# The norm of the next token group on VectorE: made a group early, in the order of the program

## Chip, cores, metric

One core of a Trainium2 chip. The metric is the device time of one execution in microseconds (us), median over runs. A profile gives a span, which is about 1.9 us shorter than the time of the same run. Line numbers such as L190 are lines of the kernel that a trace belongs to, so the same line of code has another number in each kernel.

## The reference

The output is `x + A(norm(x)) + B(norm(x))` for 2048 tokens of width 512. A is linear attention with 32 heads of width 16, B an MLP of width 1792 with the activation mish.

```
xn  = (x - mean) / sqrt(var + 1e-5)
q, k, v = split(xn @ wqkv);  pq, pk = per head q @ w_phi, k @ w_phi
phi = concat(softmax(p), softmax(-p))            # for q and k
kv  = sum over tokens of phi_k^T v;  z = sum over tokens of phi_k
A   = (phi_q @ kv / (phi_q @ z + 1e-6)) @ wo
B   = mish(xn @ w1 + b1) @ w2
```

kv and z need all tokens before any output exists. So the kernel has a first phase over 4 groups of 512 tokens (4 tiles of 128 each) and then a second phase that makes the outputs.

## The kernel before

A group of the first phase makes, on TensorE, `pk` (keys folded with w_phi), `pv` (values), `pq`, seven pairs of `ph` (the MLP) and `pkv` (the sum over tokens). ScalarE does the exponentials `ek` and `eqT` and mish. VectorE makes, for each tile, the sums `ss`, the reciprocals `rk` and the products `v12`, which `pkv` reads; it also does the norm: statistics `st`, their aggregates `mv`, the reciprocal root `rstd` (on GpSimd for groups 1 to 3), the scaled tile `xn` and its transpose `xnT` (made by a DMA for groups 1 to 3). To fold is to multiply w_phi into the weights once, at the start (`pf`); `pnd` and `po` are matmuls of the second phase. A scheduler orders the instructions of each engine, unless `follow` chains them:

```python
def follow(key, ins):            # orders ins behind the last instruction with the same key
    ...tc.add_manual_dep(ins.ins, prev.ins.name, <order only, no wait>)...

def stage_ln(g):
    ...
    for t in range(TPG):
        st = spool.tile(...)
        follow("dve", nc.vector.bn_stats(st[:], xg[:, t, :]))
        nc.vector.bn_aggr(mv[:, t, :], st[:])
    ...                          # g > 0: 1/sqrt(var + eps) of all four tiles on GpSimd
    for t in range(TPG):
        xn = xnpool.tile([P, D], BF16, name="xn")            # pool of 4
        nc.vector.tensor_scalar(out=xn[:], in0=xg[:, t, :], ...subtract mean, times rstd...)
        if g > 0:
            nc.sync.dma_start_transpose(out=xnT[:, t], in_=xn[:])

def finish(ek):                  # returned by v_pair; pvs are two PSUM banks of a pool of 2
    for tt in range(2):
        nc.vector.reduce_sum(ss[:], ek[:, :, tt, :]...)
        nc.vector.reciprocal(rk[:], ss[:])
        nc.vector.tensor_tensor(out=v12[...], in0=pvs[tt]..., in1=rk..., op=ALU.mult)

for g in range(NG):
    # [cut] g = 0: v_pair, fold of wq, two k_pair
    ek0 = k_pair(xnT, 0); ek1 = k_pair(xnT, 1)
    v0, vfin = v_pair(xnT, 0);  vfin(ek0)
    q_pair(g, xnT, 0); q_pair(g, xnT, 1)
    h_pair(xnT, acts[g], 0)
    v1, vfin = v_pair(xnT, 1);  vfin(ek1)
    if g + 1 < NG:
        xnTs[g + 1], _ = stage_ln(g + 1)                     # written here, placed by the scheduler
    for fp in range(1, 4): h_pair(xnT, acts[g], fp)
    stage_kvacc(g, parts)                                    # pkv, then kvacc on VectorE
    for fp in range(4, 7 or 6): h_pair(xnT, acts[g], fp)
```

The softmax here doesn't subtract the row's maximum and nothing guards it: scores larger than these inputs give would overflow.

Of the kernel before, what the change touches and what calls it, by code (L numbers as in the profile page):

```python
# [17 lines left out]
def kernel(  # L18
# [12 lines left out]
    nc = tc.nc  # L31
# [38 lines left out]
    nc.scalar.dma_start(wk_raw[:], wqkv_v[:, :, D : 2 * D])  # L70
    wv = wts.tile([P, KT, D], BF16, name="wv")
    nc.sync.dma_start(wv[:], wqkv_v[:, :, 2 * D : 3 * D])
    Wsrc = prep_w.tile([P, 4, DH], BF16, name="Wsrc")
    with nc.allow_non_contiguous_dma(reason="tiny w_phi load"):
        nc.scalar.dma_start(Wsrc[:], wphi_v)
# [48 lines left out]
    wqp = wts.tile([P, KT, D], BF16, name="wqp")  # L124
    wkp = wts.tile([P, KT, D], BF16, name="wkp")
# [38 lines left out]
    def rstd_of(g, rstd, mv):  # L164
        if g == 0:
            follow("act", nc.scalar.activation(rstd, mv, ACT.Sqrt, bias=eps_t[:]))
            nc.vector.reciprocal(rstd, rstd)
        else:
            nc.gpsimd.tensor_scalar(
                out=rstd, in0=mv, scalar1=1e-5, scalar2=None, op0=ALU.add  # L170
            )
            nc.gpsimd.tensor_tensor(out=rstd, in0=rstd, in1=mhalf[:], op=ALU.pow)

    def stage_ln(g):
        xg = xgs[g]
        mv = spool.tile([P, TPG, nc.vector.BN_AGGR_DIM], FP32, name="mv")
        rstd = spool.tile([P, TPG], FP32, name="rstd")
        xnT = xnTpool.tile([P, TPG, KT, P], BF16, name="xnT")
        xns = []
        for t in range(TPG):  # L180
            st = spool.tile([P, nc.vector.BN_STATS_DIM], FP32, name="st")
            follow("dve", nc.vector.bn_stats(st[:], xg[:, t, :]))  # L182
            nc.vector.bn_aggr(mv[:, t, :], st[:])
            if g == 0:
                rstd_of(g, rstd[:, t : t + 1], mv[:, t : t + 1, 1])
        if g > 0:
            rstd_of(g, rstd[:], mv[:, :, 1])
        for t in range(TPG):
            xn = xnpool.tile([P, D], BF16, name="xn")
            nc.vector.tensor_scalar(  # L190
                out=xn[:],
                in0=xg[:, t, :],
                scalar1=mv[:, t, 0:1],
                scalar2=rstd[:, t : t + 1],
                op0=ALU.subtract,
                op1=ALU.mult,
            )
            xns.append(xn)
            if g > 0:
                nc.sync.dma_start_transpose(out=xnT[:, t], in_=xn[:])  # L200
        return xnT, xns

    def ln_T(xnT, xns):
        if True:
            ptr = big("ptr", [P, TPG, KT, P], BF16)
            for t in range(TPG):
                for kt in range(KT):
                    pe(
                        nc.tensor.transpose(
                            ptr[:, t, kt, :], xns[t][:, kt * P : (kt + 1) * P], ident[:]  # L210
                        )
                    )
            nc.scalar.copy(xnT[:, 0:2], ptr[:, 0:2])
            nc.vector.tensor_copy(xnT[:, 2:4], ptr[:, 2:4])
# [11 lines left out]
    def fold_T(src, engines):  # L226
# [11 lines left out]
        for jh, copy in enumerate(engines):  # L238
            ins = copy(wT[:, 2 * jh : 2 * jh + 2, :], ptr[:, 2 * jh : 2 * jh + 2, :])
            if src is wq_raw and jh == 0:  # L240
                follow("act", ins)
        return wT

    def fold_mm(wT, dst):
        for kp in range(KT // 2):
            pf = big("pf")
            for kk in range(2):
                kt = 2 * kp + kk
                for j in range(4):
                    pe(nc.tensor.matmul(  # L250
                        pf[:, kk, j * P : (j + 1) * P],
                        lhsT=wT[:, j, kt * P : (kt + 1) * P],
                        rhs=Wbd[:, j, :],
                        start=True,
                        stop=True,
                    ))
            follow("dve", nc.vector.tensor_copy(dst[:, 2 * kp, :], pf[:, 0]))
            follow("act", nc.scalar.copy(dst[:, 2 * kp + 1, :], pf[:, 1]))


    def k_pair(xnT, pr):
        pk = big("pk")
        for tt in range(2):
            for kt in range(KT):
# [3 lines left out]
                    rhs=wkp[:, kt, :],  # L268
# [7 lines left out]

    def v_pair(xnT, pr):
        pvs = []
        for tt in range(2):
            pv = bank_v("pv")  # L280
            for kt in range(KT):
                pe(
                    nc.tensor.matmul(  # L283
                        pv[:],
                        lhsT=xnT[:, 2 * pr + tt, kt, :],
                        rhs=wv[:, kt, :],
                        start=(kt == 0),
                        stop=(kt == KT - 1),
                    )
                )  # L290
            pvs.append(pv)
        v12s = []

        def finish(ek):
            for tt in range(2):
                ss = spool.tile([P, 2, NH], FP32, name="ss")
                nc.vector.reduce_sum(  # L297
# [3 lines left out]
                )  # L301
                rk = spool.tile([P, 2, NH], FP32, name="rk")
                nc.vector.reciprocal(rk[:], ss[:])  # L303
                v12 = vpool.tile([P, 2, NH, VW], BF16, name="v12")
                nc.vector.tensor_tensor(  # L305
# [6 lines left out]
                )  # L312
# [275 lines left out]
```

## Time and profile before

| | before |
|---|---|
| time, 3 runs | 196.21 us median (195.61 to 197.53) |
| span of the profiled run, and its time | 195.2 us, 197.05 us |
| TensorE / VectorE / ScalarE busy | 181.2 / 119.0 / 107.9 us |
| mean granted TensorE clock | 0.983 |

The page's summary of the chain that ended last, by engine, reads:

```profile
PE 75%; ACT 7%; DVE 7%; DMA 5%; issue 2%; SPq 2%; POOL 1%; ACTq 0%; DVEq 0%; POOLq 0%
```

The chain is followed back from the last instruction; a share is time in which that engine (PE is TensorE, DVE is VectorE, ACT is ScalarE) held up the end. Three quarters are TensorE's own work. The prediction below shows where the rest lies. Its lines are read so: a line of the chain has start, length, engine, what; a line of the timeline adds shapes, the number of instructions, and in brackets how long the engine sat idle before and for whom; a line of the waits has the total, the number of waits and the longest. Some matmul records are missing from a trace, so a count such as x7 can stand for 8.

### The profile page before, as it was taken

To read this page: it belongs to the slowest core of one execution; us is meant where nothing else is said; L and a number is where in the kernel's file an instruction comes from. 1 tells how busy PE (TensorE), PEld (TensorE's weight loads), DVE (VectorE), ACT (ScalarE), POOL (GpSimd) and SP (SyncE) were. 2 spreads that over 40 slices of the span, in tenths; PEclk is the share of its full clock that TensorE was granted. 3 is DMA by queue.
4 is the path that set the end of the run, shared out by engine and by line. 5 is a ranking of instruction groups with operands and counts; after the bars stand their busy time and mean duration, and the time that the engine had idled before them with its cause. 6 is when DMAs were issued, how large, how long until landed. Compare 5 with 4: busy or idle time off the path is not lost.

```text
span 195.2 us, 2791 instructions
## 1 busy us (share of the span) xinstructions
PE 181.2 (93%) x1034; PEld 90.7 (46%) x1051; DVE 119.0 (61%) x233; ACT 107.9 (55%) x175; POOL 14.0 (7%) x35
## 2 busy tenths in 40 slices
PE   7779999999189999999999999999999999999992
PEld 2355446444034644446444464445555555555440
DVE  1948999364894203982039864897666677766600
ACT  3578976598704479974799855343322222333311
POOL 3200410202110000110001100000000000000000
PEclk9999999999958999999999999999999999999999
DMA  6999302619300013000000000138322632222220
GB/s 192 381 403 386 151 0 55 125 59 197 108 0 0 3 27 81 0 0 3 0 0 0 0 3 0 27 81 165 55 69 66 164 81 57 54 54 57 54 81 27
DMA packets 24233, 15.93 MB, mean 82 GB/s; under 512 B 16284, under 2 KB 23196, under 8 KB 24220
## 3 DMA queue, kind: packets, MB, share of 16 engines
q1 hardware_dynamic: 22636, 14.69, 27.4%
q10 hardware_dynamic: 1584, 1.07, 1.7%
q8 instruction: 8, 0.13, 0.3%
q14 instruction: 5, 0.04, 0.1%
HBM read 9.98 MB, written 2.10 MB: 62 GB/s over the span
## 4 chain that ended last, share of the span: by engine, by line
PE 75%; ACT 7%; DVE 7%; DMA 5%; issue 2%; SPq 2%; POOL 1%; ACTq 0%; DVEq 0%; POOLq 0%
PE ph L366 25%; PE po L453 22%; PE po L462 6%; PE pv L283 6%; PE pk L265 4%; PE pkv L326 4%; DMA Wsrc<-in_A_w_phi_dram 4%; PE pq L348 4%; PE pnd L390 4%; SPq L200 2%; ACT ek L274 1%; ACT ek L273 1%; ACT act L377 1%; DMA xnT<-xn 1%; DVE ss L297 1%
## 5 line engine op out<-in xcount | busy, mean ns | idle before, releaser
L366 PE MATMUL ph<-xnT,w_sb 128*128 128x512 bf16 x224 | 51.8, 386 | 0.4 <-ACT eqT L357 0.4
L453 PE MATMUL po<-w_sb,act 128*128 128x512 bf16 x216 | 51.2, 379 | 0.4
L377 ACT ACTIVATE act<-ph,b1f 128x512 bf16<-128x512 f32 x56 | 35.5, 684 | 27.4 <-PE ph L366 27.4
L366 PEld LDWEIGHTS <-w_sb 128*128 128x128 bf16 x224 | 22.2, 100 | 27.1 <-issue 2.9
L471 ACT CAST y<-po 128x512 bf16<-128x512 f32 x16 | 9.4, 586 | 44.4 <-PE po L462 44.4
L453 PEld LDWEIGHTS <-act 128*128 128x128 bf16 x224 | 21.3, 98 | 22.3
L297 DVE TENSOR_REDUCE ss<-ek 128x64 f32<-128x1024 bf16 x16 | 18.7, 1211 | 19.1 <-ACT ek L274 19.0
L422 DVE TENSOR_TENSOR on<-pnd,wd 128x512 f32<-128x512 f32 x32 | 20.6, 686 | 1.7
L283 PE MATMUL pv<-wv,xnT 128*128 128x512 bf16 x59 | 16.4, 408 | 5.0 <-DVE v L305 4.6
L305 DVE TENSOR_TENSOR v<-pv,rk 128x1024 bf16<-128x1024 f32 x16 | 18.3, 1188 | 0.0
L462 PE MATMUL po<-wo_sb,oT 128*128 128x512 bf16 x63 | 16.4, 379 | 0.1
L357 ACT ACTIVATE eqT<-pq 128x1024 bf16<-128x1024 f32 x16 | 15.1, 1040 | 0.7 <-PE pq L348 0.6
L182 DVE BATCH_NORM_STATS2 st<-xg 128x6 f32<-128x512 bf16 x16 | 10.4, 672 | 8.1 <-DMA xg<-in_A_x_dram 8.1
L348 PE MATMUL pq<-xnT,wqp 128*128 128x512 bf16 x64 | 14.5, 379 | 0.0
L265 PE MATMUL pk<-wkp,xnT 128*128 128x512 bf16 x61 | 14.3, 379 | 0.2
L407 DVE TENSOR_TENSOR td<-ds 128x64 f32<-128x64 f32 x16 | 3.6, 225 | 16.4 <-ACT ds L403 16.3
L283 PEld LDWEIGHTS <-xnT 128*128 128x128 bf16 x64 | 6.5, 103 | 13.0 <-issue 6.6
L390 PE MATMUL pnd<-kvm,eqT 128*128 128x144 bf16 x128 | 11.3, 226 | 0.5 <-DVE on L422 0.3
L390 PEld LDWEIGHTS <-eqT 128*128 128x128 bf16 x128 | 9.0, 98 | 5.9 <-DVE on L422 2.4
L313 POOL CAST v<-rk 128x64 bf16<-128x64 f32 x16 | 7.0, 458 | 64.5 <-DVE rk L303 64.5
L429 DVE TENSOR_TENSOR o_t<-on 128x512 bf16<-128x512 f32 x16 | 11.1, 692 | 0.5
L338 DVE TENSOR_TENSOR kvacc<-pkv,kvacc 128x544 f32<-128x544 f32 x6 | 4.3, 725 | 9.9 <-PE pkv L326 9.9
(63 smaller groups left out, 150.1 us busy)
## 6 DMA issues: line engine op xcount, KB each, us to landing
xg<-in_A_x_dram SPq DMA_DIRECT2D x8, 512.0 KB, 4.1
out_dram<-y SPq DMA_DIRECT2D x16, 128.0 KB, 2.1
w_sb<-in_B_w_dram SPq DMA_DIRECT2D x2, 896.0 KB, 9.9
w_sb<-in_B_w_dram SPq DMA_DIRECT2D x1, 1792.0 KB, 12.9
wk_raw<-in_A_wqkv_dram ACTq DMA_DIRECT2D x1, 512.0 KB, 5.1
wv<-in_A_wqkv_dram SPq DMA_DIRECT2D x1, 512.0 KB, 6.0
wq_raw<-in_A_wqkv_dram ACTq DMA_DIRECT2D x1, 512.0 KB, 10.1
wo_sb<-in_A_wo_dram SPq DMA_DIRECT2D x1, 512.0 KB, 13.5
```

The costliest lines, as they stand in the source:

```text
L265: pe(nc.tensor.matmul(pk[:, tt, :], lhsT=xnT[:, 2 * pr + tt, kt, :], rhs=wkp[:, kt, :], start=(kt == 0), stop=(kt == KT - 1),))
L283: nc.tensor.matmul(pv[:], lhsT=xnT[:, 2 * pr + tt, kt, :], rhs=wv[:, kt, :], start=(kt == 0), stop=(kt == KT - 1),)
L297: nc.vector.reduce_sum(ss[:], ek[:, :, tt, :].rearrange("p s (h e) -> p s h e", e=DH), axis=AX.X,)
L305: nc.vector.tensor_tensor(out=v12[:, :, :, 0:DH], in0=pvs[tt][:] .rearrange("p (o h e) -> p o h e", o=1, e=DH) .to_broadcast([P, 2, NH, DH ...
L348: pe(nc.tensor.matmul(pq[:, jj, :], lhsT=wqp[:, kt, j * P : (j + 1) * P], rhs=xnT[:, :, kt, :], start=(kt == 0), stop=(kt == KT - 1),))
L357: follow("act", nc.scalar.activation(eqT[:, sl, gs], pq[:], ACT.Exp, scale=sign))
L366: nc.tensor.matmul(ph[:, ff, :], lhsT=w1_sb[:, kt, f * P : (f + 1) * P], rhs=xnT[:, :, kt, :], start=(kt == 0), stop=(kt == KT - 1),)
L377: nc.scalar.activation(act[:, f, :], ph[:, ff, :], ACT.Mish, bias=b1f[:, f : f + 1])
L390: nc.tensor.matmul(pnd[:, j // 2, (j % 2) * 144 : (j % 2) * 144 + 144], lhsT=eqT[:, pl * 4 + j, tok0 : tok0 + P], rhs=kvm[:, pl * 4 + j], ...
L422: nc.vector.tensor_tensor(out=on[:, pl], in0=nds[pl][:, :, :, 0:DH], in1=wd[:, pl, :, :, None].to_broadcast([P, 2, 16, DH]), op=ALU.mult,)
L453: nc.tensor.matmul(po[:], lhsT=acts[g][:, f, t * P : (t + 1) * P], rhs=w2_sb[:, f, :], start=False, stop=False, skip_group_check=True,)
L462: nc.tensor.matmul(po[:], lhsT=oT[:, j, :], rhs=wo_sb[:, j, :], start=False, stop=(j == 3), skip_group_check=True,)
```

## The change

Its intent is to give VectorE's idle time to the norm: the norm of group g+1 is written at the head of group g, all VectorE instructions of the first phase are chained in the order of the program, and group 0 is written out tile by tile so that its parts mesh. The mask copy into `kvm` moves into group 0, group 0's accumulation stands one h pair later, and the load of w_phi changes its issuing engine.

```diff
-    wv load on sync;  Wsrc (w_phi) load on scalar, behind wk
+    Wsrc (w_phi) load on sync, behind x;  then the wv load
 class Norm:                                     # replaces stage_ln and ln_T
+        def stats(self, t):
+            follow("dve", nc.vector.bn_stats(...)); follow("dve", nc.vector.bn_aggr(...))
+        def write(self):
+            for t in range(TPG):
+                self.scale(t)                   # follow("dve", tensor_scalar)
+                nc.sync.dma_start_transpose(out=self.xnT[:, t], in_=self.xns[t][:])
         def finish(ek, tts=(0, 1)):
-            nc.vector.reduce_sum(...)
+            follow("dve", nc.vector.reduce_sum(...))     # and so reciprocal, product, kvacc
+    # group 0: stats, root, invert, scale, transposes, folds, k, v in a set order (cut)
     for g in range(NG):
+        if g > 0 and g + 1 < NG:
+            nn = Norm(g + 1); xnTs[g + 1] = nn.xnT
+            nn.measure(); nn.write()            # at the head of group g
         ...
+        if g == 0:
+            nn = Norm(1); nn.measure(); vfin(ek1, (0,)); nn.write(); vfin(ek1, (1,))
-        if g + 1 < NG:
-            xnTs[g + 1], _ = stage_ln(g + 1)
+        if g + 2 < NG:                          # x is loaded a group earlier too
+            xgs[g + 2] = xpool.tile(...); nc.sync.dma_start(xgs[g + 2][:], x_g[g + 2])
+        cut = 5 if g == 0 else 4
-        for fp in range(1, 4): h_pair(...)
+        for fp in range(1, cut): h_pair(...)
```

More of the change, by code (lines that the diff above doesn't have):

```diff
@@ L70 @@
     nc.scalar.dma_start(wk_raw[:], wqkv_v[:, :, D : 2 * D])
+    Wsrc = prep_w.tile([P, 4, DH], BF16, name="Wsrc")
+    with nc.allow_non_contiguous_dma(reason="tiny w_phi load"):
+        nc.sync.dma_start(Wsrc[:], wphi_v)
     wv = wts.tile([P, KT, D], BF16, name="wv")
     nc.sync.dma_start(wv[:], wqkv_v[:, :, 2 * D : 3 * D])
-    Wsrc = prep_w.tile([P, 4, DH], BF16, name="Wsrc")
-    with nc.allow_non_contiguous_dma(reason="tiny w_phi load"):
-        nc.scalar.dma_start(Wsrc[:], wphi_v)
     wq_raw = prep_w.tile([P, KT, D], BF16, name="wq_raw")
@@ L123 @@
     b1f = wts.tile([P, FT], FP32, name="b1f")
-    wqp = wts.tile([P, KT, D], BF16, name="wqp")
-    wkp = wts.tile([P, KT, D], BF16, name="wkp")
+    wqp = [wts.tile([P, 2, D], BF16, name="wqp%d" % i) for i in range(2)]
+    wkp = [wts.tile([P, 2, D], BF16, name="wkp%d" % i) for i in range(2)]
     eqT = persist.tile([P, 8, S], BF16, name="eqT")
@@ L161, in bank_v @@
         return ps_v.tile(shape or [P, 512], dt, name=name, tag="v")
-    def rstd_of(g, rstd, mv):
-        if g == 0:
-            follow("act", nc.scalar.activation(rstd, mv, ACT.Sqrt, bias=eps_t[:]))
-            nc.vector.reciprocal(rstd, rstd)
-        else:
-            nc.gpsimd.tensor_scalar(
-                out=rstd, in0=mv, scalar1=1e-5, scalar2=None, op0=ALU.add
-            )
-            nc.gpsimd.tensor_tensor(out=rstd, in0=rstd, in1=mhalf[:], op=ALU.pow)
-    def stage_ln(g):
-        xg = xgs[g]
-        mv = spool.tile([P, TPG, nc.vector.BN_AGGR_DIM], FP32, name="mv")
-        rstd = spool.tile([P, TPG], FP32, name="rstd")
-        xnT = xnTpool.tile([P, TPG, KT, P], BF16, name="xnT")
-        xns = []
-        for t in range(TPG):
-            st = spool.tile([P, nc.vector.BN_STATS_DIM], FP32, name="st")
-            follow("dve", nc.vector.bn_stats(st[:], xg[:, t, :]))
-            nc.vector.bn_aggr(mv[:, t, :], st[:])
-            if g == 0:
-                rstd_of(g, rstd[:, t : t + 1], mv[:, t : t + 1, 1])
-        if g > 0:
-            rstd_of(g, rstd[:], mv[:, :, 1])
-        for t in range(TPG):
-            xn = xnpool.tile([P, D], BF16, name="xn")
-            nc.vector.tensor_scalar(
-                out=xn[:],
-                in0=xg[:, t, :],
-                scalar1=mv[:, t, 0:1],
-                scalar2=rstd[:, t : t + 1],
-                op0=ALU.subtract,
-                op1=ALU.mult,
-            )
-            xns.append(xn)
-            if g > 0:
-                nc.sync.dma_start_transpose(out=xnT[:, t], in_=xn[:])
-        return xnT, xns
@@ L203, in ln_T, with __init__, root_act, invert @@
-    def ln_T(xnT, xns):
-        if True:
-            ptr = big("ptr", [P, TPG, KT, P], BF16)
-            for t in range(TPG):
+    class Norm:
+        def __init__(self, g):
+            self.xg = xgs[g]
+            self.mv = spool.tile([P, TPG, nc.vector.BN_AGGR_DIM], FP32, name="mv")
+            self.rstd = spool.tile([P, TPG], FP32, name="rstd")
+            self.xnT = xnTpool.tile([P, TPG, KT, P], BF16, name="xnT")
+            self.xns = {}
+        def stats(self, t):
+            st = spool.tile([P, nc.vector.BN_STATS_DIM], FP32, name="st")
+            follow("dve", nc.vector.bn_stats(st[:], self.xg[:, t, :]))
+            follow("dve", nc.vector.bn_aggr(self.mv[:, t, :], st[:]))
+        def root_act(self, t):
+            rs = self.rstd[:, t : t + 1]
+            follow(
+                "act",
+                nc.scalar.activation(rs, self.mv[:, t, 1:2], ACT.Sqrt, bias=eps_t[:]),
+            )
+        def invert(self, t):
+            rs = self.rstd[:, t : t + 1]
+            follow("dve", nc.vector.reciprocal(rs, rs))
+        def scale(self, t):
+            xn = xnpool.tile([P, D], BF16, name="xn")
+            follow(
+                "dve",
+                nc.vector.tensor_scalar(
+                    out=xn[:],
+                    in0=self.xg[:, t, :],
+                    scalar1=self.mv[:, t, 0:1],
+                    scalar2=self.rstd[:, t : t + 1],
+                    op0=ALU.subtract,
+                    op1=ALU.mult,
+                ),
+            )
+            self.xns[t] = xn
+        def turn(self, th):
+            ptr = (big if th else bank_v)("ptr", [P, 2, KT, P], BF16)
+            for t in range(2):
@@ L209, in ln_T, with root_all, measure @@
                         nc.tensor.transpose(
-                            ptr[:, t, kt, :], xns[t][:, kt * P : (kt + 1) * P], ident[:]
-                        )
-                    )
-            nc.scalar.copy(xnT[:, 0:2], ptr[:, 0:2])
-            nc.vector.tensor_copy(xnT[:, 2:4], ptr[:, 2:4])
+                            ptr[:, t, kt, :],
+                            self.xns[2 * th + t][:, kt * P : (kt + 1) * P],
+                            ident[:],
+                        )
+                    )
+            follow(
+                "dve", nc.vector.tensor_copy(self.xnT[:, 2 * th : 2 * th + 2], ptr[:])
+            )
+        def root_all(self):
+            nc.gpsimd.tensor_scalar(
+                out=self.rstd[:],
+                in0=self.mv[:, :, 1],
+                scalar1=1e-5,
+                scalar2=None,
+                op0=ALU.add,
+            )
+            nc.gpsimd.tensor_tensor(
+                out=self.rstd[:], in0=self.rstd[:], in1=mhalf[:], op=ALU.pow
+            )
+        def measure(self):
+            for t in range(TPG):
+                self.stats(t)
+            self.root_all()
+        def write(self):
+            for t in range(TPG):
+                self.scale(t)
+                nc.sync.dma_start_transpose(out=self.xnT[:, t], in_=self.xns[t][:])
     Wbd = prep_w.tile([P, 4, P], BF16, name="Wbd")
@@ L224, with act_copy, dve_copy, fold_T @@
         )
-    def fold_T(src, engines):
+    def act_copy(out, in_):
+        follow("act", nc.scalar.copy(out, in_))
+    def dve_copy(out, in_):
+        follow("dve", nc.vector.tensor_copy(out, in_))
+    def fold_T(src):
         ptr = big("ptrw", [P, 4, 512], BF16)
@@ L237, in fold_T, with half, fold_mm @@
                 )
-        for jh, copy in enumerate(engines):
-            ins = copy(wT[:, 2 * jh : 2 * jh + 2, :], ptr[:, 2 * jh : 2 * jh + 2, :])
-            if src is wq_raw and jh == 0:
-                follow("act", ins)
-        return wT
-    def fold_mm(wT, dst):
-        for kp in range(KT // 2):
-            pf = big("pf")
-            for kk in range(2):
-                kt = 2 * kp + kk
-                for j in range(4):
-                    pe(nc.tensor.matmul(
-                        pf[:, kk, j * P : (j + 1) * P],
+        return ptr, wT
+    def half(t, jh):
+        return t[:, 2 * jh : 2 * jh + 2, :]
+    def fold_mm(pfs, wT, js):
+        for kt in range(KT):
+            for j in js:
+                pe(
+                    nc.tensor.matmul(
+                        pfs[kt // 2][:, kt % 2, j * P : (j + 1) * P],
                         lhsT=wT[:, j, kt * P : (kt + 1) * P],
@@ L255, in fold_mm @@
                         stop=True,
-                    ))
-            follow("dve", nc.vector.tensor_copy(dst[:, 2 * kp, :], pf[:, 0]))
-            follow("act", nc.scalar.copy(dst[:, 2 * kp + 1, :], pf[:, 1]))
+                    )
+                )
     def k_pair(xnT, pr):
@@ L267, in k_pair @@
                     lhsT=xnT[:, 2 * pr + tt, kt, :],
-                    rhs=wkp[:, kt, :],
+                    rhs=wkp[kt // 2][:, kt % 2, :],
                     start=(kt == 0),
@@ L275, in k_pair, with v_tile, v_use, finish @@
         return ek
-    def v_pair(xnT, pr):
-        pvs = []
-        for tt in range(2):
-            pv = bank_v("pv")
-            for kt in range(KT):
-                pe(
-                    nc.tensor.matmul(
-                        pv[:],
-                        lhsT=xnT[:, 2 * pr + tt, kt, :],
-                        rhs=wv[:, kt, :],
-                        start=(kt == 0),
-                        stop=(kt == KT - 1),
-                    )
-                )
-            pvs.append(pv)
+    def v_tile(xnT, t):
+        pv = bank_v("pv")
+        for kt in range(KT):
+            pe(
+                nc.tensor.matmul(
+                    pv[:],
+                    lhsT=xnT[:, t, kt, :],
+                    rhs=wv[:, kt, :],
+                    start=(kt == 0),
+                    stop=(kt == KT - 1),
+                )
+            )
+        return pv
+    def v_pair(xnT, pr):
+        return v_use([v_tile(xnT, 2 * pr + tt) for tt in range(2)])
+    def v_use(pvs):
         v12s = []
-        def finish(ek):
-            for tt in range(2):
+        def finish(ek, tts=(0, 1)):
+            for tt in tts:
                 ss = spool.tile([P, 2, NH], FP32, name="ss")
-                nc.vector.reduce_sum(
+                follow("dve", nc.vector.reduce_sum(
                     ss[:],
@@ L300, in finish @@
                     axis=AX.X,
-                )
+                ))
                 rk = spool.tile([P, 2, NH], FP32, name="rk")
-                nc.vector.reciprocal(rk[:], ss[:])
+                follow("dve", nc.vector.reciprocal(rk[:], ss[:]))
                 v12 = vpool.tile([P, 2, NH, VW], BF16, name="v12")
-                nc.vector.tensor_tensor(
+                follow("dve", nc.vector.tensor_tensor(
                     out=v12[:, :, :, 0:DH],
@@ L311, in finish @@
                     op=ALU.mult,
-                )
+                ))
                 nc.gpsimd.tensor_copy(v12[:, :, :, DH], rk[:])
@@ L335, in stage_kvacc @@
             if g == 0:
-                nc.vector.tensor_copy(acc, src)
+                follow("dve", nc.vector.tensor_copy(acc, src))
             else:
-                nc.vector.tensor_tensor(out=acc, in0=src, in1=acc, op=ALU.add)
+                follow(
+                    "dve",
+                    nc.vector.tensor_tensor(out=acc, in0=src, in1=acc, op=ALU.add),
+                )
     def q_pair(g, xnT, jp):
@@ L349, in q_pair @@
                         pq[:, jj, :],
-                        lhsT=wqp[:, kt, j * P : (j + 1) * P],
+                        lhsT=wqp[kt // 2][:, kt % 2, j * P : (j + 1) * P],
                         rhs=xnT[:, :, kt, :],
@@ L484 @@
         )
-    xnTs[0], xns0 = stage_ln(0)
-    wkT = fold_T(wk_raw, (nc.scalar.copy, nc.scalar.copy))
-    ln_T(xnTs[0], xns0)
-    fold_mm(wkT, wkp)
-    wqT = fold_T(wq_raw, (nc.scalar.copy, nc.vector.tensor_copy))
-    follow("act", nc.scalar.activation(warm[:], eps_t[:], ACT.Exp))
+    n0 = Norm(0)
+    xnTs[0] = n0.xnT
+    ptk, wkT = fold_T(wk_raw)
+    n0.stats(0)
+    n0.root_act(0)
+    n0.stats(1)
+    n0.root_act(1)
+    for t in range(2):
+        n0.invert(t)
+        n0.scale(t)
+    act_copy(half(wkT, 0), half(ptk, 0))
+    n0.stats(2)
+    n0.root_act(2)
+    act_copy(half(wkT, 1), half(ptk, 1))
+    n0.turn(0)
+    n0.stats(3)
+    n0.root_act(3)
+    for t in range(2, 4):
+        n0.invert(t)
+        n0.scale(t)
+    pfk = [big("pf"), big("pf")]
+    fold_mm(pfk, wkT, (0, 1))
+    pv0 = v_tile(xnTs[0], 0)
+    fold_mm(pfk, wkT, (2, 3))
+    act_copy(wkp[0][:], pfk[0][:])
+    dve_copy(wkp[1][:], pfk[1][:])
+    v0, vfin = v_use([pv0, v_tile(xnTs[0], 1)])
+    n0.turn(1)
+    ptq, wqT = fold_T(wq_raw)
+    dve_copy(half(wqT, 0), half(ptq, 0))
+    dve_copy(half(wqT, 1), half(ptq, 1))
+    follow("act", nc.scalar.activation(warm[:], eps_t[:], ACT.Exp))
+    ek0 = k_pair(xnTs[0], 0)
+    pfq = [big("pf"), big("pf")]
+    fold_mm(pfq, wqT, (0, 1, 2, 3))
+    dve_copy(wqp[0][:], pfq[0][:])
+    act_copy(wqp[1][:], pfq[1][:])
+    ek1 = k_pair(xnTs[0], 1)
     for g in range(NG):
         xnT = xnTs[g]
-        if g == 0:
-            v0, vfin = v_pair(xnT, 0)
-            fold_mm(wqT, wqp)
-            ek0 = k_pair(xnT, 0)
-            ek1 = k_pair(xnT, 1)
-        else:
+        if g > 0:
+            if g + 1 < NG:
+                nn = Norm(g + 1)
+                xnTs[g + 1] = nn.xnT
+                nn.measure()
+                nn.write()
             ek0 = k_pair(xnT, 0)
@@ L507 @@
             nc.tensor.transpose(pb[:], b1row[:], ident[0:FT, 0:FT])
-            nc.vector.tensor_copy(b1f[:], pb[:])
+            follow("dve", nc.vector.tensor_copy(b1f[:], pb[:]))
+            follow(
+                "dve",
+                nc.vector.tensor_copy(
+                    kvm[:, :, :, VW], mask17[:, None, :, 0].to_broadcast([P, 8, 8])
+                ),
+            )
             prep_w.release()
@@ L519 @@
         v1, vfin = v_pair(xnT, 1)
-        vfin(ek1)
-        parts = [(ek0, v0), (ek1, v1)]
-        if g + 1 < NG:
-            if g + 1 > 1:
-                xgs[g + 1] = xpool.tile([P, TPG, D], BF16, name="xg")
-                nc.sync.dma_start(xgs[g + 1][:], x_g[g + 1])
-            xnTs[g + 1], _ = stage_ln(g + 1)
-        for fp in range(1, 4):
+        if g == 0:
+            nn = Norm(1)
+            xnTs[1] = nn.xnT
+            nn.measure()
+            vfin(ek1, (0,))
+            nn.write()
+            vfin(ek1, (1,))
+        else:
+            vfin(ek1)
+        parts = [(ek0, v0), (ek1, v1)]
+        if g + 2 < NG:
+            xgs[g + 2] = xpool.tile([P, TPG, D], BF16, name="xg")
+            nc.sync.dma_start(xgs[g + 2][:], x_g[g + 2])
+        cut = 5 if g == 0 else 4
+        for fp in range(1, cut):
             h_pair(xnT, acts[g], fp)
         stage_kvacc(g, parts)
-        for fp in range(4, 7 if g + 1 < NG else 6):
+        for fp in range(cut, 7 if g + 1 < NG else 6):
             h_pair(xnT, acts[g], fp)
-    nc.vector.tensor_copy(
-        kvm[:, :, :, VW], mask17[:, None, :, 0].to_broadcast([P, 8, 8])
-    )
     kvv = kvacc[:].rearrange("p s (h v) -> p s h v", v=VW)
```

## The prediction

> **What bounds the kernel now.** I read the page first, then the chain of waits in order of time, then the waits, the timeline of VectorE and a table by stage. On the page TensorE is busy for 93% of the span, so only its holes and slow stretches can be won. Rows of engine and granted clock, in 40 slices of 4.88 us:
>
> ```profile
> PE   7779999999189999999999999999999999999992
> ...
> DVE  1948999364894203982039864897666677766600
> ...
> PEclk9999999999958999999999999999999999999999
> ```
>
> There is one hole, in slice 10 (TensorE at 1, VectorE at 8), with a clock of 5 and 8 tenths after it. The start (slices 0 to 2) is less than full too. The chain around the hole:
>
> ```profile
> 49.44 0.41 DVE xn L190
> 49.85 2.25 DVE ss L297 x2
> 52.11 0.52 DVE rk L303 x2
> 52.63 0.27 issue
> 52.90 1.17 DVE v L305
> 54.07 0.04 issue
> 54.11 1.44 PE pv L283 x3
> ...
> 71.20 0.21 PE pk L265
> ...
> 95.54 0.21 PE pk L265
> ```
>
> TensorE waits for `v` of group 1, which stands behind the sums `ss`, which stand behind an `xn` scale. The waits from 39 to 60 us say how long:
>
> ```profile
> DVE st L182 <- DMA xg<-in_A_x_dram: 4.8, 1, 4.8
> PE pv L283 <- DVE v L305: 4.6, 1, 4.6
> DVE xn L190 <- DMA xnT<-xn: 3.6, 3, 2.4
> ```
>
> And whose scale it is, from the timeline of VectorE:
>
> ```profile
> 40.53 0.69 DVE L182 BATCH_NORM_STATS2 st<-xg 128x6 f32<-128x512 bf16 x1 [4.75 <-DMA xg<-in_A_x_dram]
> 47.08 0.83 DVE L190 TENSOR_SCALAR xn<-xg,mv,rstd 128x512 bf16<-128x512 bf16 x2 [2.44 <-DMA xnT<-xn]
> 49.44 0.41 DVE L190 TENSOR_SCALAR xn<-xg,mv,rstd 128x512 bf16<-128x512 bf16 x1 [0.88 <-DMA xnT<-xn]
> ```
>
> These are the statistics and scales of **group 3**, two groups ahead. The scheduler pulled them in front of group 1's sums. The first waits for x to land; the scales wait until the transposes of group 2 have read the four `xn` buffers. The exponentials of tile pair 0 were ready at 43.72; the sums started at 49.77. About 6 us of VectorE's time were given to work needed 50 us later.
>
> The hole costs twice. The table by stage:
>
> ```profile
> 54.11:57.50 3.39, 3.17 (x8) 1.16 (x9) 3.39 (x4) 0.00 (x0) 0.00 (x0) 0.50 0.00 0
> 57.50:60.00 2.50, 2.50 (x7) 0.86 (x6) 2.50 (x4) 0.00 (x0) 0.87 (x2) 0.50 0.00 0
> 71.20:95.54 24.34, 24.23 (x135) 12.09 (x136) 12.21 (x14) 18.98 (x24) 1.74 (x4) 1.00 0.11 22
> ```
>
> (Columns: stretch, length, busy of PE, PEld, DVE, ACT, POOL, granted clock, DMA share, GB/s.) From 54.11 to 60.04 the clock is 0.50: 14 matmuls of 512 columns at about 0.427 us apart instead of 0.216 (24 of L366 in 5.18 us). That is 14 x 0.211 = 2.95 us. Check by periods: group 2 takes 24.34 us from its first pk to the next group's; group 1 takes 32.04 (38.99 to 71.03 in the timeline). The excess is 7.70 = 4.60 + 2.95 + 0.15.
>
> **What the Trainium skill says.** (1) "TensorE: Matmul & The Clock Gate", Part 1, the two states: the array falls to half rate after an idle window of about 3.4 us and comes back after a window of about that length sustained busy; the window runs freely. The trace agrees in kind: after a wait of 4.60 us the clock is 0.50, though it lasted 5.93 us. Waits of 0.4 to 1.1 us at the start had no drop. (2) "PSUM — Partial Sum Buffer", Engine vs sequencer instructions: the VectorE queue is strict FIFO. The trace agrees: sums whose inputs were ready at 43.72 stood until 49.77. So the order in the program, not readiness, decides. (3) "DMA: Bandwidth & Descriptors", Issuing engines are not separate DMA queues: loads of both issuing engines share the same 16 DMA engines. So moving w_phi's load to the other queue changes whose turn it is, not the sum; nothing here shows that before the run.
>
> **The change, part by part.** I read the new order on each engine from the built program.
>
> *A. Order in groups 1 to 3.* VectorE now does group g+1's statistics and scales at the head of group g, in front of group g's sums, and nothing of g+2. Each group's VectorE list: 4 statistics with their aggregates (0.67 and 0.17 us, dependent pairs about 0.85, so 3.4), GpSimd's root (0.23 + 1.04, with hand-overs about 1.5), 4 scales (1.37 in the trace), then sums. Does that fit in the idle time? The last accumulation of the previous group ends about 0.9 us after its pkv. After pkv come 2 h pairs (3.46 us) in group 1, 3 (5.19) in group 2; the exponentials are ready 4.7 us after the first pk (38.99 to 43.72). So room is 7.3 us in group 1 and 9.0 in group 2, for 3.4 + 1.5 + 1.4 = 6.3. It fits, with 1.0 us in the tighter case. Then sums, reciprocals and products of two tiles take 5.42 us (19.60 to 25.02), done 10.1 us after the first pk, while the second pv tile needs the bank at 24 + 16 + 8 matmuls and one more tile, 11.2 us after. Slack 1.1 us. The whole excess goes: **-7.7 us**. Groups 2 and 3 were already without a hole (24.23 busy of 24.34), so they gain nothing.
>
> *B. Group 0's start.* The same transposes, folds and copies are interleaved tile by tile; copies become 1024 wide and the second half no longer waits for all four tiles. My estimate with the trace's durations, assuming x lands at 4.57 as before: xn 0 and 1 done 7.4; the first half of xnT 8.9; first `wT` half 8.0; folds and the first v tile to 10.5; folded key weights in SBUF by 11.9 on VectorE (1.2 us for 1024 elements); wq's transposes 11.9 to 12.9; first pk 12.9; its exponentials 14.8 to 16.7; the copy of wqp on ScalarE to 17.7; second pk 16.8 (it waits for a PSUM buffer) and exponentials 18.6 to 20.5; four of q from 20.5. First h at about 22.4 instead of 23.28: **-0.8 us**, unsure by 0.6. The bound there is ScalarE's row of exponentials in both kernels.
>
> *C. Group 0's VectorE row.* Before, group 1's statistics ran at 16.7 to 19.5, while VectorE had nothing else. Now they come after the first sums, behind the b1 copy and the mask copy. From 16.7: sums of pair 0 5.4 (22.1), b1 and mask copies 0.7 (22.9), statistics 3.4 (26.3), one tile 2.7 (29.0), scales 1.4 (30.4), last tile 2.7: 33.1. TensorE: h 0 from 22.4 (1.73), seven v matmuls (1.5), four h pairs (6.9): at pkv by 32.6. The cut at 5 instead of 4 gives those 1.73 us. A wait of about 0.5 us remains, too short for the clock. Then rest of pkv with one v matmul of group 1 moved among it (2.1), two h pairs (3.46): group 1's pk at about 38.7 instead of 38.99: **-0.3 us net of B**. Transposes of group 1 (four issues in 5.22 us, landing 2.5 later) start at 29.5 and are in by 36 to 37, before 38.7.
>
> *D. Loads and the rest.* w_phi in front of wv on the queue of x may cost wv up to 1 us (it landed at 7.25 and is now needed at 9.0) and should free wq, which landed at 11.93 with TensorE waiting 1.1. I count nothing. The tail from the first pnd is unchanged.
>
> Sum: -7.7 - 0.3, and 0.2 for a v matmul of group 1 done already: -8.2 us. **196.2 - 8.2 = 188.0 us.**
>
> **The rivals.** (1) *The hole moves rather than goes.* VectorE in group 0 is now full from 16.7 to 33.1 and the pkv waits for its last v; if the first exponentials come 1 us later than I put them, the wait grows by that much, and beyond 3 us the clock would fall again (another 3). For it: the list is serial. Against: the cut at 5 shows that this was balanced. Result 189 to 191. (2) *The new norm in front of the sums delays them in group 1.* The slack is 1.0 us, then 1.1 more at pv. A root on GpSimd 2 us slower, or x of group 2 late, would make a wait of about 1 us; result 189. x of group 2 landed before 31.6 in the old trace, so it is unlikely. (3) *The start is slower*, as wv or w_phi lands late, or many short waits of TensorE hold the clock at half: +1 to +3 us, 189 to 191. (4) *The clock falls for a cause of its own*, so that only 4.6 us are won: 191. Against: the only slow stretch follows the only long wait.
>
> **Range and chances.** The low end, 186.3: the hole of group 1 goes whole, and the start keeps B and a further 0.9 us (no wait in C, wq early). Rivals 1 and 3 together: 190.3. For less than 2% (above 192.3) more than half of A must fail, which takes a new hole of over 3 us. Chances: faster 0.95, same 0.04, slower 0.01.
>
> **What would show it.** Right: no wait of `pv` for `v` above 1 us; granted clock 1.00 from 40 to 70 us; first pk of group 1 and of group 2 24.3 us apart; first h near 22.4; a wait of pkv for the last v in group 0 of 0 to 1 us; TensorE busy about 178 us (181.2 - 2.95). Wrong: a clock near 0.5 anywhere after 10 us, or a wait of over 2 us of VectorE for `xg` or for transposes in front of sums.

## The result

The changed kernel takes 189.2 us (median of 4, 189.07 to 189.3); before, in the same rounds and those above, 195.91 us (median of 4, 194.9 to 197.53). The ratio is 0.965, with a 95% interval of 0.958 to 0.972. A ratio is the mean time of one kernel's runs over that of the other's of the same rounds, so it is not quite the ratio of these medians. It is clearly faster, by 6.7 us on the medians, and inside the range (186.3 to 190.3); the centre predicted was 188.0.

The page of the changed kernel, the rows that answer to those of before (slices of 4.68 us now), and the chain by engine:

```profile
PE   7898999899999999999999999999999999999992
...
DVE  1997999757978359930299738996666666666600
...
PEclk9999999999999999999999999999999999999999
...
PE 70%; DVE 19%; ACT 4%; DMA 4%; issue 1%; SPq 0%; DVEq 0%; ACTq 0%
```

The hole and the stretch of slow clock are gone. But the chain runs over VectorE for 19% of the span now, 7% before: the chain of waits shows where. That share is not what could be won: once a wait, however short, leads the chain to VectorE, all its work back to its own input is counted.

```profile
31.96 1.24 DVE v L334
33.20 0.05 issue
33.25 1.71 PE pkv L355 x26
...
38.41 3.45 PE pk L291 x16
...
62.54 3.47 PE pk L291 x16
...
72.55 1.24 DVE v L334
73.79 0.04 issue
73.83 1.02 PE pv L307 x4
...
87.11 3.47 PE pk L291 x16
```

From the first `pk` of group 1 to that of group 2 it is 24.13 us here (32.04 in the timeline of before), all of it TensorE's work. In groups 0, 2 and 3 TensorE waits for a `v` product, 0.5 us in group 0 and 0.2 to 0.4 in the others. What stands on VectorE at the head of group 1 is now the norm of group 2, and it is done before the exponentials:

```profile
40.40 1.38 DVE L192 TENSOR_SCALAR xn<-xg,mv,rstd 128x512 bf16<-128x512 bf16 x4 [1.48 <-POOL rstd L226]
43.00 1.22 DVE L326 TENSOR_REDUCE ss<-ek 128x64 f32<-128x1024 bf16 x1 [1.22 <-ACT ek L300]
```

The sums waited 1.22 us for ScalarE; before, they stood 6 us behind group 3's scales. The stretches that had the slow clock, and the longer period of group 2:

```profile
54.11:57.50 3.39, 3.39 (x41) 2.57 (x39) 1.99 (x3) 2.19 (x4) 0.42 (x1) 1.00 0.00 0
57.50:60.00 2.50, 2.50 (x14) 1.08 (x12) 2.43 (x6) 0.88 (x2) 0.00 (x0) 1.00 0.02 7
62.54:87.11 24.57, 24.50 (x137) 12.04 (x136) 14.54 (x18) 18.96 (x24) 2.05 (x5) 1.00 0.17 43
```

Clock 1.00 in both, but group 2 takes 24.57 us where it took 24.34. The account by TensorE's timeline, in us:

| stage | before | after | difference |
|---|---|---|---|
| start to first pk of group 1 | 38.99 | 38.25 | -0.74 |
| group 1 | 32.04 | 24.12 | -7.92 |
| group 2 | 24.34 | 24.58 | +0.24 |
| group 3, pk to the h behind pkv | 19.16 | 19.63 | +0.47 |
| rest | 80.67 | 80.62 | -0.05 |
| span | 195.2 | 187.2 | -8.0 |

### The profile page after: what moved, and what is told of

Its sections match the earlier page's. It is cut to its first block, busy times and chain, and to the rows that moved or that the text cites. A ratio compares the mean times of both kernels' runs of the same rounds, so it can differ in the third digit from the quotient of the medians.

```text
span 187.2 us, 2803 instructions
## 1 busy us (share of the span) xinstructions
PE 179.4 (96%) x1051; PEld 89.8 (48%) x1051; DVE 125.4 (67%) x233; ACT 105.8 (57%) x171; POOL 14.4 (8%) x35
## 4 chain that ended last, share of the span: by engine, by line
PE 70%; DVE 19%; ACT 4%; DMA 4%; issue 1%; SPq 0%; DVEq 0%; ACTq 0%
PE po L485 23%; PE ph L398 19%; PE pk L291 6%; PE po L494 6%; DVE v L334 5%; DVE ss L326 5%; PE pkv L355 4%; PE pv L307 4%; DMA wv<-in_A_wqkv_dram 4%; PE pnd L422 4%; DVE rk L332 2%; PE pq L380 2%; ACT ek L300 1%; DVE st L174 1%; ACT ek L299 1%
## 5 line engine op out<-in xcount | busy, mean ns | idle before, releaser
L485 PE MATMUL po<-w_sb,act 128*128 128x512 bf16 x224 | 51.8, 379 | 0.0
L398 PE MATMUL ph<-xnT,w_sb 128*128 128x512 bf16 x224 | 50.5, 379 | 0.0
L326 DVE TENSOR_REDUCE ss<-ek 128x64 f32<-128x1024 bf16 x16 | 19.4, 1211 | 14.4 <-ACT ek L300 14.4
L334 DVE TENSOR_TENSOR v<-pv,rk 128x1024 bf16<-128x1024 f32 x16 | 19.6, 1227 | 1.5
L479 ACT CAST po<-xg 128x512 f32<-128x512 bf16 x16 | 10.0, 624 | 1.4 <-DVE v L334 1.4
L435 ACT COPY ds<-pnd 128x64 f32<-128x64 f32 x32 | 8.7, 280 | 3.0 <-PE pnd L422 3.0
```

The source lines that it names most:

```text
L326: follow("dve", nc.vector.reduce_sum(ss[:], ek[:, :, tt, :].rearrange("p s (h e) -> p s h e", e=DH), axis=AX.X,))
L334: follow("dve", nc.vector.tensor_tensor(out=v12[:, :, :, 0:DH], in0=pvs[tt][:] .rearrange("p (o h e) -> p o h e", o=1, e=DH) .to_broadcast ...
L398: nc.tensor.matmul(ph[:, ff, :], lhsT=w1_sb[:, kt, f * P : (f + 1) * P], rhs=xnT[:, :, kt, :], start=(kt == 0), stop=(kt == KT - 1),)
L485: nc.tensor.matmul(po[:], lhsT=acts[g][:, f, t * P : (t + 1) * P], rhs=w2_sb[:, f, :], start=False, stop=False, skip_group_check=True,)
```

## The experiments

The theory: one misplaced block on VectorE (group 3's norm in front of group 1's sums) makes the whole loss of group 1, first as a hole of TensorE and then as a slow clock. Rivals: the new start or the set order of VectorE is what counts; the place of the norm in the program is enough; the slow clock has a cause of its own. All outputs were correct.

| run | time, median us | ratio to before |
|---|---|---|
| one_edge | 189.14 (4 runs) | 0.963 |
| free_order | 194.45 (4) | 0.990 |
| late_strict | 199.01 (4) | 1.015 (95% interval 1.007 to 1.023) |
| warm_hole | 194.08 (4) | 0.988 |
| before, same rounds | 196.53 (7) | 1 |
| cut4 | 190.29 (6) | 0.971 |
| pairs | 188.25 (6) | 0.9605 |
| wphi_act | 189.54 (6) | 0.967 |
| pairs_stats | 187.86 (6) | 0.958 |
| before, same rounds | 196.19 (11) | 1 |
| start_edge | 188.58 (6) | 0.963 |
| changed kernel again | 189.23 (6) | 0.966 |
| one_edge again | 189.24 (6) | 0.967 |
| pairs_stats again | 187.89 (6) | 0.959 |
| before, same rounds | 195.55 (11) | 1 |

The three blocks are on three chips. What ran on two of them agrees within 0.1 us (one_edge 189.14 and 189.24, pairs_stats 187.86 and 187.89), so differences of 0.3 us and more between the blocks are read below.

### One order edge in the kernel before

```diff
-            follow("dve", nc.vector.bn_stats(st[:], xg[:, t, :]))
+            ins = follow("dve", nc.vector.bn_stats(st[:], xg[:, t, :]))
+            if g == 3 and t == 0:    # order only: behind group 1's last v product
+                tc.add_manual_dep(ins.ins, last_v[1].ins.name, <order only, no wait>)
```

> The kernel before with one order edge added: the first statistics of group 3 may not stand on VectorE before the last v product of group 1. Start, group 0 and all else as before. Theory (group 3's norm hoisted in front of group 1's sums makes the hole, and the hole makes the slow clock): the 4.6 us wait of pv for v and the stretch at clock 0.50 go, span about 195.2 - 7.6 = 187.6, time 188.8 to 189.8, as good as the whole change within 0.5 us. Rival (the gain needs the set order everywhere and the new start): at least half of the loss stays, time 192 or more.

Measured: 189.14 us, equal to the whole change. The chain of waits in group 1 is TensorE's own work from end to end; where the hole was, it reads:

```profile
47.61 1.73 PE ph L377 x8
49.34 0.65 PE pv L294 x3
```

So one edge gives what the whole change gives. The rest of the change adds up to nothing, which does not yet say that each part is worth nothing.

### The norm early in the program, but the order free

```diff
+    loose = [False]
+    def fd(ins):                 # used for aggregates, scales, sums, reciprocals, products, kvacc
+        return ins if loose[0] else follow("dve", ins)
             vfin(ek1, (1,))
+            loose[0] = True      # from the end of group 0's v products on
```

> The changed kernel with its norm a group early in the program as it is, but without the order edges on VectorE after group 0 (only the statistics keep theirs, as in the kernel before). The built order puts group 3's norm in front of group 1's sums again; it is the same instruction order on all engines as the changed kernel with the norm written late and free. Theory: the wait of pv for v in group 1 is back at 4 to 5 us, with a stretch at clock 0.50, time 195 to 197. Rival A (the place in the program is what matters): 189. Rival B (the new start is worth several us of the gain): 191 to 193.

Measured: 194.45 us. VectorE's timeline (group 3's scale, then group 1's sums), the waits and a stage of the table, same columns as in the prediction:

```profile
48.14 0.41 DVE L195 TENSOR_SCALAR xn<-xg,mv,rstd 128x512 bf16<-128x512 bf16 x1 [0.86 <-DMA xnT<-xn]
48.47 2.34 DVE L329 TENSOR_REDUCE ss<-ek 128x64 f32<-128x1024 bf16 x2
```

```profile
PE pv L310 <- DVE v L337: 4.0, 1, 4.0
```

```profile
52.80:58.00 5.20, 4.97 (x12) 1.89 (x13) 5.20 (x6) 0.00 (x0) 0.87 (x2) 0.50 0.00 0
```

Hole and slow clock are back: the scheduler put group 3's norm in front of group 1's sums once more, though in the program it stands a group behind them. The place in the program is not enough; the edge is. The time is 0.5 us under the range that I gave; it is 2.1 us under before, of which the earlier start (first pk of group 1 at 38.49, 0.5) and the shorter hole (4.0 for 4.6) are 1.1. The rest is the clock's: three of its four runs had a mean clock of 0.99, and two of the seven of before (the two lots are told below). Its three runs at 0.99 have a mean of 194.25 us and those of before 195.3; its run at 0.98 took 195.37 and those of before 196.6. So like runs differ by 1.1 to 1.2.

### The set order, but the norm late

```diff
         if g > 0:
-            if g + 1 < NG: nn = Norm(g + 1); ...; nn.measure(); nn.write()
     ...
         else:
             vfin(ek1)
+            if g + 1 < NG: nn = Norm(g + 1); ...; nn.measure(); nn.write()
```

> The changed kernel with the order of VectorE set as it is, but the norm of the next group written behind the last v product of groups 1 and 2 instead of at their head. Theory (order and earliness are both needed): xn of group 2 would be done at about 60.5 us and its transposes land 62 to 67, while the next pk can start at 62.4; TensorE waits 1 to 4 us at the head of groups 2 and 3 each, and accumulation waits too; time 191 to 196, waits of pk for the transposes. Rival (a set order alone is enough): 189.2 within 0.5.

Measured: 199.01 us, slower than I had put it, and for another reason than the transposes. Waits from 55 to 70 us, VectorE's timeline, and the table of the stretch after:

```profile
PE ph L398 <- DVE kvacc L369: 3.1, 1, 3.1
```

```profile
60.24 1.38 DVE L192 TENSOR_SCALAR xn<-xg,mv,rstd 128x512 bf16<-128x512 bf16 x4 [1.48 <-POOL rstd L226]
61.54 1.35 DVE L369 TENSOR_TENSOR kvacc<-pkv,kvacc 128x544 f32<-128x544 f32 x2
```

```profile
62.31:67.40 5.09, 5.09 (x13) 1.78 (x13) 0.58 (x1) 1.26 (x2) 0.00 (x0) 0.50 0.53 100
```

The accumulation `kvacc` stood behind the scales, and the scales waited 1.48 us for GpSimd's root. Until `kvacc` has read it, the PSUM tile of `pkv` is not free, and the next h pair waits for it: 3.05 us in group 1, 2.95 in group 2, each followed by a slow clock (0.50, and 0.72 on average from 92.9 to 97.6). Here the set order with the block in the wrong place is worse than the free one (2.5 us slower than before; the record calls it unclear). A set order is not enough, then: the place in it counts. One_edge leaves the norm where before has it in the program, keeps group 3's norm behind group 1's products and leaves the rest to the scheduler, which runs group 3's statistics between group 1's last products and `kvacc` and splits the scales around it.

### The hole kept, the clock kept up

```diff
+        if g == 1:
+            pd = big("pd")               # PSUM tile that nobody reads
+            for i in range(20):
+                nc.tensor.matmul(pd[:, i % 2], lhsT=zero[:, 0:P], rhs=zero[:], start=True, stop=True)
         v1, vfin = v_pair(xnT, 1)
```

> The kernel before with 20 dummy matmuls of 512 columns (of zeros, into a PSUM tile that nobody reads) on TensorE in front of the second v pair of group 1, in the hole. The hole stays as long: v comes at the same time. Theory (the second half of the loss is the clock falling after the idle time): the clock stays 1.00, span 195.2 - 2.9 = 192.3, time about 193.5, and the spread from run to run, 194.9 to 197.5 before, falls below 0.6 us, as it is the length of the slow stretch that varies. Rival (the slow clock has a cause of its own): a stretch at 0.50 somewhere from 50 to 65 us stays, time 195.5 to 197.

Measured: 194.08 us, and four runs within 0.34 us. TensorE's timeline behind the dummy matmuls (49.28 to 53.76), and the stretch from there in the table:

```profile
53.84 2.15 PE L283 MATMUL pv<-wv,xnT 128*128 128x512 bf16 x8
```

```profile
53.90:60.00 6.10, 6.00 (x28) 2.64 (x28) 6.10 (x7) 1.78 (x3) 0.87 (x2) 1.00 0.00 0
```

The second `pv` pair starts about as late as before (53.84 and 54.11; `v` still comes last, at 53.80), but the clock stays at 1.00. So the fall of the clock comes from the idle time, and it costs 196.53 - 194.08 = 2.4 us; the hole itself costs 194.08 - 189.14 = 4.9 us. The spread belongs to the clock too. The 29 runs of before fall into two lots by the mean granted clock: 16 runs at 0.98, mean 196.6 us (196.05 to 198.15), and 13 at 0.99, mean 195.3 us (194.99 to 195.56). Kernels without the slow stretch spread by 0.2 to 0.6 us, but for one run of one_edge at 190.75, whose mean clock was 0.991. It has no trace, so what slowed it is not known.

The traces show what the lots are. In finer steps of the table the clock is at 0.50 from 53.27 to 60.10 us in before, 51.28 to 58.10 in free_order, 61.40 to 68.23 and 92.12 to 95.54 in late_strict: three times 6.83 us and once 3.42, half of it. If one stretch makes the whole loss of mean clock, 0.982 over 194.7 us is 2 x 0.018 x 194.7 = 7.0 us at half clock, and 0.991 over 193.7 us is 3.5. So the two lots fit the two lengths; only a run of the longer kind was traced for before.

### Group 0's accumulation one h pair earlier

```diff
-        cut = 5 if g == 0 else 4
+        cut = 4
```

> The changed kernel with group 0's accumulation again behind three h pairs instead of four (cut 4 instead of 5). Theory (group 0 is bound by VectorE's serial list, whose last v comes at 33.2 us whatever TensorE does): TensorE reaches the accumulation 1.73 us earlier, waits 2.2 to 2.6 us for the last v instead of 0.8, and group 1 starts 1.7 us later: time 190.7 to 191.1; the clock should hold[...]. Rival (group 0 is bound by TensorE and the cut is idle tuning): 189.2.

Measured: 190.29 us, 1.06 more than the changed kernel. The wait for `v` itself is gone from the trace, as the scheduler filled its place: v matmuls of group 1 (3 in the records, 4 by their time) and 4 of the h pair now stand among `pkv`. The first of these waited 0.95 us for the transposes of group 1, which come from VectorE's scales, in the same list.

```profile
32.16 1.04 PE L307 MATMUL pv<-wv,xnT 128*128 128x512 bf16 x3 [0.95 <-DMA xnT<-xn]
...
33.89 1.70 PE L355 MATMUL pkv<-v,ek 128*128 128x136 bf16 x26
```

Right in kind (reaching the accumulation earlier wins nothing; VectorE's list decides), too large in size (1.7 predicted, 1.06 measured).

### A v pair step by step instead of tile by tile

```diff
         def finish(ek, tts=(0, 1)):
-            for tt in tts: sum; reciprocal; product
+            for tt in tts: sum
+            for tt in tts: reciprocal
+            for tt in tts: product               # all still chained with follow("dve", ...)
```

> The changed kernel with the two tiles of a v pair taken step by step (both sums, both reciprocals, both products) instead of tile by tile, still in a set order; group 0's second pair stays split by the norm. Theory (tile by tile every VectorE instruction waits for the one before it, which makes 6.1 us of a pair that took 5.42 in the kernel before; that costs TensorE 0.8 us at group 0's accumulation and about 0.24 us at the second v pair of groups 2 and 3 each): these waits go, time 188.2 to 188.6, and the wait of pv for v in groups 2 and 3 is 0. Rival (the bubbles lie in idle time): 189.2 within 0.2.

Measured: 188.25 us. VectorE at group 2's first pair, in the changed kernel and then in this one:

```profile
67.60 1.22 DVE L326 TENSOR_REDUCE ss<-ek 128x64 f32<-128x1024 bf16 x1 [3.42 <-ACT ek L300]
68.85 0.55 DVE L332 RECIPROCAL rk<-ss 128x64 f32<-128x64 f32 x1
...
73.69 1.21 DVE L326 TENSOR_REDUCE ss<-ek 128x64 f32<-128x1024 bf16 x1
```

```profile
67.69 2.35 DVE L327 TENSOR_REDUCE ss<-ek 128x64 f32<-128x1024 bf16 x2 [3.42 <-ACT ek L300]
...
73.03 2.33 DVE L327 TENSOR_REDUCE ss<-ek 128x64 f32<-128x1024 bf16 x2
```

The same six instructions take 73.69 - 67.60 = 6.09 us in one order and 73.03 - 67.69 = 5.34 in the other. The waits of `pv` for `v` in groups 2 and 3 are gone (group 2 takes 24.34 us again, as in before, and group 3's stretch 19.16), and the wait of `pkv` in group 0 fell from 0.5 to 0.3 us. This was a cost of the change itself: the kernel before had left these instructions to the scheduler, which paired them.

### The load of w_phi put back

```diff
-    nc.sync.dma_start(Wsrc[:], wphi_v)      # behind x, in front of wv
+    nc.scalar.dma_start(Wsrc[:], wphi_v)    # behind wk, in front of wq
```

> The changed kernel with the load of w_phi put back where it was, behind wk on the other issuing engine's queue. Theory (the move of the load is worth a little): w_phi lands at 8.3 instead of 6.2 us, wv at 7.3 instead of 8.8, wq at 11.9 instead of 8.5; the first h starts 0.2 to 0.8 us later and the time is 189.3 to 189.9. Rival (wv is what the start waits for, so that the move cost time): 188.6 to 189.1.

Measured: 189.54 us (189.46 to 189.68), 0.3 more than the changed kernel. w_phi landed 6.9 us after its issue instead of 4.9, wq 10.0 instead of 7.2, wv 6.2 instead of 7.1; the first fold waited 0.86 us for GpSimd, which waits for w_phi, and the first h started at 22.50, where three traces with the load moved have 22.16 to 22.27 (pairs_stats, pairs, cut4); the changed kernel's first trace, with 21.89, is the earliest of all. The move of the load is worth a little, as the theory says.

### Pairs, and aggregates one tile behind the statistics

```diff
-            for t in range(TPG): stats(t) then aggregate(t)
+            for t in range(TPG + 1): stats(t) if t < TPG; aggregate(t - 1) if t > 0
```

> As pairs, and the aggregates of groups 1 to 3 one tile behind their statistics, so that they do not wait for them. Theory: VectorE's list in group 0 is 0.4 us shorter still, but by then TensorE is late at the accumulation rather than VectorE: 0 to 0.2 us better than pairs, 188.0 to 188.5. Rival (VectorE still bounds group 0): 0.4 us better than pairs.

Measured: 187.86 us, 0.4 better than pairs, which is the rival's figure: VectorE still bound group 0 in pairs, by the 0.3 us that `pkv` waited. With both, no wait of TensorE for `v` is left from group 0 to group 3.

### The new start with one edge, and the best once more

start_edge is free_order with the edge of one_edge.

> The new start and group 0 of the changed kernel, but no set order on VectorE in groups 1 to 3 except the one edge of the run one_edge (group 3's first statistics behind group 1's last v). Theory (the new start is worth about 0.6 us at group 1's first pk, and tile by tile order takes back about 0.5 us in groups 2 and 3): 188.6 to 188.8, that is 0.4 to 0.6 better than both the changed kernel and one_edge on the same chip. Rival (the start is worth nothing): 189.1 to 189.3.

> The changed kernel itself once more, as the measure for the other runs on this chip: 189.0 to 189.4.

> The kernel before with the one edge, once more, beside the changed kernel on the same chip: equal to it within 0.2 us.

> The best version so far beside the changed kernel on the same chip: 1.2 to 1.5 us faster than it, 187.7 to 188.0.

Measured on one chip: start_edge 188.58 us, the changed kernel 189.23, one_edge 189.24, pairs_stats 187.89. So the new start and group 0 are worth 189.24 - 188.58 = 0.66 us, and the set, tile by tile order of groups 1 to 3 takes back 189.23 - 188.58 = 0.65 us: that is why one edge equals the whole change. The best version is 1.3 us under the changed kernel.

## Why the prediction was right, and by how much it was off

- **Part A, the cause.** Right, and shown by experiment: one edge that holds back group 3's norm gives the gain (one_edge), and the changed kernel without its edges in groups 1 to 3 loses it, though the norm stands early in the program (free_order). A set order alone does not give it: with the norm behind the v products, other holes open (late_strict). Group 1 became 7.92 us shorter, where part A (7.7) and the moved v matmul (0.2) make 7.9.
- **Part A, the two halves of the loss.** Right in kind, a little large in the clock's half: 2.95 us read from one trace, 2.4 us on the medians (warm_hole), 2.5 and 1.3 us for the two lots of before. The clock fell at 53.27 us, before TensorE went on at 54.11, so it was at half for 6.83 us, not for the 5.93 that the prediction read from the matmuls. That a wait must pass 3 us for the clock to fall, as rival 1 has it, did not hold: it fell in a wait of 2.95 (late_strict).
- **Part A, groups 2 and 3 "gain nothing".** They lose 0.24 and 0.47 us. The term that was mis-sized is the 5.42 us for two tiles, taken from a trace where the instructions were paired; in the order of the change they take 6.09. I had read that the change goes tile by tile and kept the old duration. Besides, the exponentials of group 2 were ready 5.2 us after its first pk, not 4.7. The slack of 1.1 us was not there. In pairs, with 5.34 us, both losses are gone.
- **Part B, the start.** Right in kind, a little small: first h at 21.89 us, and 22.00 to 22.27 in the other traces with this start; predicted 22.4; 23.11 to 23.28 in the traces with the old one. w_phi came at 6.2 us and wq no longer held TensorE (1.1 us before), for which I had counted nothing; wphi_act shows 0.3 us of it.
- **Part C, group 0's VectorE list.** The last v ended at 33.20 us, predicted 33.1, and pkv waited 0.5, as predicted. That it fits so closely is luck, as errors cancel inside: the first pair took 6.0 us for 5.4 and the two single tiles 3.0 and 3.1 for 2.7, but the list began 0.3 us earlier, the b1 and mask copies took 0.3 for 0.7 and the statistics 3.1 for 3.4.
- **The sum.** The span fell by 8.0 us, predicted 8.2. The time fell by less, since I subtracted from the median of 196.2 what I had read in the trace of a run of 197.05, one of those with the longer slow stretch. That last step is 0.85 us of the 1.2 by which 188.0 missed 189.2. A trace and the number from which its savings are taken must be of the same run. Two slips besides: 22.1 and 0.7 make 22.8, not 22.9, and the parts named for the low end (7.7, 0.2, 0.8 and 0.9) lead to 186.6, not 186.3.
- **The rivals.** None came true. Rival 1: the wait of pkv stayed at the 0.5 us of part C. Rival 2 (the norm delays the sums in group 1): they waited 1.22 us for ScalarE. Rival 3: the start came earlier. Rival 4: the clock went with the hole.
- **Signs.** All that were named as right came, but one: TensorE was busy for 179.4 us, not about 178. The trace of before has 17 matmul records fewer (1034 for 1051), so its 181.2 us is likely too low; this is not settled.
- **Open:** what decides which of the two lengths a slow stretch has, and the one slow run of one_edge (190.75).

## What to carry to other kernels

When a scheduler places instructions, look on the waiting engine's timeline for work that is needed much later, and first try one order edge that keeps it back: here one edge was worth as much as a rewritten group. If you chain a whole engine by hand, chain it so that neighbours do not depend on each other, and keep what frees a PSUM tile in front of long blocks. The hole of 4.6 us in TensorE cost about half as much again in slow clock behind it (2.4 us for 4.9), and waits of 2.95 and 3.05 us brought a slow clock too; a few dummy matmuls in a hole show how much.

## What the Trainium skill lacked or had wrong

- "TensorE: Matmul & The Clock Gate", Part 1, the two states, has the array fall to half rate after an idle window of about 3.4 us, and the table in its section "Why this matters for your kernels" sets the limit at about 3 us. Here it fell in waits of 3.05 and 2.95 us too (late_strict), and there 2.1 and 2.2 us after TensorE's last matmul; in before it was 3.8. For the way back Part 1 asks for one such busy window or more, which agrees: 0.50 lasted 3.42 or 6.83 us, one window or two. The page does not say that the cost so comes in two sizes (runs of 195.3 and 196.6 us).
- The same page does not say whether matmuls of zeros count as activity. They do here: 20 of them in the hole kept the clock at 1.00 (warm_hole).
- "VectorE: DVE Perf Modes", Rules for kernel authors, advises for chained operations to reduce their count, not their semaphores. With count and work unchanged, putting independent instructions between dependent ones took two tiles from 6.09 to 5.34 us (pairs). Whether the wait itself or the data dependence makes the gap, no run here separates.
- No page says that hand-set order can lose what a scheduler's pairing gives: 0.65 us in groups 1 to 3 (start_edge against the changed kernel).
